# A planner's rule for two engines that share a way into memory, a shorter mask, a scalar add and a split last copy

## The chip, the cores and the metric

The kernel runs on one core of a Trainium2 chip. A core has a matrix engine (TensorE, in the profile PE, with its weight loads as PEld), VectorE (DVE), ScalarE (ACT), GpSimd (POOL) and SyncE (SP), which here issues all the DMAs. Each engine works through its own queue of instructions in order and waits on semaphores for the others. Operands lie in on-chip memory (SBUF), matmul results in PSUM, which is held as eight banks of 128 x 512 words.

The metric is the device time of one execution in microseconds (us), taken over three runs. Their median before the change is 683.23.

## The reference

Attention with a few sink positions and a sliding window, followed by a two-layer network whose activation is the squared positive part. Batch 4, 8 heads, 768 positions, head size 64; 4 sinks and a window of 128; model size 512, inner size 2048.

```python
scores = scale * np.matmul(q, k.transpose(0, 1, 3, 2))
is_sink = pos[None, :] < int(n_sink)
rel = pos[:, None] - pos[None, :]
in_window = (rel >= 0) & (rel < int(window))
scores = np.where(is_sink | in_window, scores, -1000000000.0)
a = np.exp(scores - np.max(scores, axis=-1, keepdims=True))
a = a / (np.sum(a, axis=-1, keepdims=True) + 1e-09)
attn = np.matmul(a, v)
...
x = attn.transpose(0, 2, 1, 3).reshape(B * S, H * D)
h = np.maximum(x @ w_in, 0.0)
return (h * h @ w_out)
```

Queries and keys are float32; the network's weights come as 64-bit floats and are unpacked on the chip.

## The kernel before, in words

**Work.** The 3072 rows of tokens are cut into eight chunks of 384 (two to a batch). For each chunk four pairs of heads go through attention, which leaves x as a high part and a low part; then 16 steps of the network follow, each with 12 first products (L824, x by w_in), the activation (L837, L841, L846, L853) and nine second products (L869) into banks that gather the output. Three products stand for one in both layers: high by high, low by high and high by low.

**Weights.** 32 rows of weights (`row_steps`) are each loaded as 128 x 512 pairs of words, made into 32-bit floats by three DVE passes (L318 with one tensor operand, L325 and L332 with two), copied to a high part by ACT (L338), and a low part is taken by a two-operand subtraction (L342) on DVE or POOL, whichever the planner finds sooner. Most of this falls into the first 125 us.

**Attention.** The first eight pairs (`plain`) take scores straight from q and k (L501). The later 24 first split k and q into high and low parts: a one-operand cast of k on DVE (L459), a two-operand subtraction on POOL (L464), a copy of q on ACT (L470), a two-operand subtraction on DVE (L475), then L507. For each block of 128 queries a DVE instruction adds the mask and takes the row's extreme (L484), ACT exponentiates and sums (L490), DVE adds the small term to the sums and inverts (`recip`, L548 and L549), and each block is scaled by a one-operand pass (L556; ACT's form is L554). The sink columns are copied by POOL (L572), and a low part is subtracted by POOL (L570). Early pairs are then turned by PE (L684, L616), later ones by DVE (L714) and a round trip of DMAs; L772 and L776 multiply by v; L788 and L793 write x.

**Masks.** Three masks exist: `mask0` for the first block of a sequence, `mask1` for the second and `maskA` for the others. They are made once from two index ramps of POOL and the two parameters that a DMA brings, by a run of DVE passes (L221 to L257) and one POOL copy.

**Order.** Every step above is added to a planner with the engines that may do it, a cost in us, a rank, what it reads and writes, and the PSUM bank that it takes. `Plan.order` plays the engines' clocks forward and, each time, emits the step that can start soonest, by rank among those within 0.03 us; among engines for one step it takes the one that would end soonest by its queue and cost. The result is only an order: on the chip each engine goes through its list and waits for semaphores. Steps marked "port" on DVE, and every step of POOL, push each other back in that clock: a step may not start before the last such step of the other engine has had half its cost (`SHARE` is 0.5).

```python
if e == "POOL" or "port" in kind:
    t = max(t, port["DVE" if e == "POOL" else "POOL"])
...
if e == "POOL" or "port" in kind:
    port[e] = t + SHARE * cost
```

**End.** `evacuate` copies the output banks to SBUF (L910) and sends them (L923). The last bank goes in two halves, one copied by DVE and one by ACT, into the same SBUF room, and the second copy is made to wait for the first. After its last DMA issue SP reads a flag, and the engines leave the program.

Of the kernel before, what the change touches and what calls it, by code (L numbers as in the profile page):

```python
# [53 lines left out]
class Plan:  # L54
# [45 lines left out]
    def order(self):  # L100
        free = dict(PE=0.0, DVE=5.5, ACT=1.5, POOL=5.0, SP=0.5)
        port, landed, mode, flow = {"DVE": 0.0, "POOL": 0.0}, [], 0, 0.0
        open_ = [n for n, s in enumerate(self.steps) if s["waits"] == 0]
        while open_:
            best = {}
            for n in open_:
# [8 lines left out]
                if e == "POOL" or "port" in kind:  # L115
                    t = max(t, port["DVE" if e == "POOL" else "POOL"])
                best.setdefault(e, []).append((t, s["rank"], n, cost, kind, picks))
# [44 lines left out]
def sink_window_attention_moe(  # L162
# [25 lines left out]
    with ExitStack() as fast:  # L188
# [23 lines left out]
        mask1 = wp.tile([P, BAND], F32, name="mask1")  # L212
# [6 lines left out]
        )  # L219
        parf = sb("gl1", [P, 2, 2], F32, "parf")  # L220
# [7 lines left out]
        reli = sb("G0", [P, 2 * P], I32, "reli")  # L228
        nc.gpsimd.iota(reli, pattern=[[-1, 2 * P]], base=P, channel_multiplier=1)
        rel = sb("ob0", [P, 2 * P], F32, "rel")  # L230
        nc.vector.tensor_copy(rel, reli)
        coli = sb("gh1", [P, P], I32, "coli")
        nc.gpsimd.iota(coli, pattern=[[1, P]], base=0, channel_multiplier=0)
        col = sb("f0", [P, P], F32, "col")
        nc.vector.tensor_copy(col, coli)

        inw = sb("ob1", [P, 2 * P], F32, "inw")
        nc.vector.tensor_scalar(inw, rel, win, None, op0=ALU.is_lt)
        ge = sb("f1", [P, 2 * P], F32, "ge")
        nc.vector.tensor_scalar(ge, rel, 0.0, None, op0=ALU.is_ge)  # L240
        nc.vector.tensor_tensor(inw, inw, ge, op=ALU.mult)
        snk = sb("f2", [P, P], F32, "snk")
        nc.vector.tensor_scalar(snk, col, ns, None, op0=ALU.is_lt)

        def additive(dst, src):
            nc.vector.tensor_scalar(dst, src, -1.0, BIG, op0=ALU.add, op1=ALU.mult)

        either = sb("G1", [P, P], F32, "either")
# [44 lines left out]
        def bank(key):  # L293
            return banks[plan.got[key]]
# [588 lines left out]
        def evacuate(c, f0, f1, t, okey, n):  # L883
# [9 lines left out]
            if c == NCHUNK - 1 and t == NQ - 1:  # L893
                halves = [slice(0, DM // 2), slice(DM // 2, DM)]
# [311 lines left out]
```

## Time and profile before

| | |
|---|---|
| median of three runs | 683.23 us (682.70 to 684.23) |
| the profiled execution's own time | 682.0 us |
| its span in the profile | 679.8 us |
| PE busy | 659.6 us, 97% |
| DVE busy | 460.5 us, 68% |
| ACT busy | 374.1 us, 55% |
| POOL busy | 211.9 us, 31% |
| first 10 us, PE busy | 4.97 us |

The profile shows one execution. Shares over the whole span mix stages: DVE is nearly full up to 125 us and about 60% busy after 205, so the stretches are read one by one. PE's matmuls are pipelined and their ends are modelled. The trace names an instruction by its line, its engine and the tiles that it writes and reads, then its shape; "x" is a count, and in grouped rows the busy time in us and the mean in ns follow, then the idle time before it and what ended that.

### The profile page before, as it was taken

How to read it: one execution, taken by the hardware profiler on the slowest of the kernel's cores; microseconds unless marked ns; L12 is line 12 of the kernel's file. 1: busy time of each engine (PE TensorE's matmuls, PEld its weight loads, DVE VectorE, ACT ScalarE, POOL GpSimd, SP SyncE). 2: the span in 40 equal slices, each digit the busy share in tenths (PEclk: the TensorE clock that was granted, in tenths of full speed). 3: DMA queues.
4: the chain of work that ended last, by engine and by line, in shares of the span. 5: the costliest groups of instructions: out<-in, count | busy, mean ns of one | idle time of the engine just before them, and what ended most of it. 6: DMA issues, size and time to landing. Idle time of an engine off the chain costs nothing.

```text
span 679.8 us, 11460 instructions
## 1 busy us (share of the span) xinstructions
PE 659.6 (97%) x3662; PEld 573.2 (84%) x3662; DVE 460.5 (68%) x1221; ACT 374.1 (55%) x1070; POOL 211.9 (31%) x383
## 2 busy tenths in 40 slices
PE   5999899999999999999999999999999999999996
PEld 4667788898888888988888898888889888899985
DVE  7999999878888676666667666666767754242221
ACT  5887543356454444556666666666657565542221
POOL 3646443244444333223234422323332331000000
PEclk9999999999999999999999999999999999999999
DMA  7957567016868543466556767546547754310001
GB/s 242 251 168 196 174 206 218 1 37 181 243 179 226 164 133 113 126 206 187 172 153 189 220 181 219 160 144 200 171 159 210 204 164 135 124 62 1 1 0 52
DMA packets 62549, 104.93 MB, mean 154 GB/s; under 512 B 10800, under 2 KB 39216, under 8 KB 62480
## 3 DMA queue, kind: packets, MB, share of 16 engines
q1 hardware_dynamic: 62480, 104.11, 52.0%
q8 instruction: 31, 0.51, 0.3%
q14 instruction: 38, 0.31, 0.1%
HBM read 78.72 MB, written 24.38 MB: 152 GB/s over the span
## 4 chain that ended last, share of the span: by engine, by line
PE 84%; DVE 10%; ACT 2%; DMA 2%; issue 1%; POOL 1%; SPq 0%; DVEq 0%; ACTq 0%
PE bank L869 36%; PE bank L824 35%; PE bank L772 5%; PE bank L507 5%; DVE f L332 2%; DVE f L325 2%; PE bank L776 1%; PE bank L501 1%; DMA PT<-via 1%; DVE P L484 1%; DVE f L318 1%; DVE bank L846 1%; DVE w L342 1%; DVE gl L853 1%; PE bank L684 1%
## 5 line engine op out<-in xcount | busy, mean ns | idle before, releaser
L824 PE MATMUL bank<-x,w 128*128 128x384 f32 x1536 | 301.8, 338 | 0.6 <-DVE gl L853 0.6
L824 PEld LDWEIGHTS bank<-x,w 128*128 128x128 f32 x1536 | 265.9, 188 | 8.9 <-issue 1.0
L869 PE MATMUL bank<-w,gh 128*128 128x512 f32 x768 | 242.5, 397 | 0.5 <-DVE ob L910 0.5
L869 PEld LDWEIGHTS bank<-w,gh 128*128 128x128 f32 x768 | 138.8, 188 | 23.2 <-issue 1.4
L869 PE MATMUL bank<-w,gl 128*128 128x512 f32 x384 | 152.1, 396 | 0.3 <-DVE gl L853 0.3
L464 POOL TENSOR_TENSOR KS<-kn,KS 128x396 fp32r<-128x396 f32 (+1 forms) x48 | 65.0, 1355 | 238.4 <-DVE KS L459 200.8
L837 ACT ACTIVATE r<-bank 128x384 f32<-128x384 f32 x128 | 62.5, 489 | 123.3 <-PE bank L824 122.2
L846 DVE TENSOR_TENSOR bank<-bank,r 128x384 f32<-128x384 f32 x128 | 71.9, 562 | 81.0 <-ACT r L837 80.6
L490 ACT ACTIVATE P<-P,nbs 128x260 f32<-128x260 f32 (+1 forms) x192 | 93.7, 488 | 58.5 <-DVE nbs L484 57.3
L556 POOL TENSOR_SCALAR P<-P,small 128x260 f32<-128x260 f32 (+1 forms) x169 | 84.6, 516 | 63.7 <-DVE small L549 47.4
L869 PEld LDWEIGHTS bank<-w,gl 128*128 128x128 f32 x384 | 72.1, 188 | 18.1 <-DVE gl L853 1.4
L853 DVE TENSOR_TENSOR gl<-bank,gh 128x384 fp32r<-128x384 f32 x128 | 71.2, 556 | 19.8 <-ACT gh L841 10.6
L484 DVE CUSTOM_DVE_ANT_0 P<-bank,maskA 128x260 f32<-128x260 f32 x128 | 52.7, 419 | 46.5 <-PE bank L507 46.1
L841 ACT ACTIVATE gh<-r 128x384 fp32r<-128x384 f32 x128 | 66.8, 522 | 3.5 <-PE bank L869 1.0
L714 DVE STREAM_TRANSPOSE T<-P 128x384 f32<-128x384 f32 x96 | 45.3, 495 | 25.1 <-POOL P L556 23.7
L507 PEld LDWEIGHTS bank<-KS,QS 128*128 128x128 f32 x288 | 52.3, 188 | 5.8
L507 PE MATMUL bank<-KS,QS 128*128 128x260 f32 (+1 forms) x288 | 55.1, 277 | 0.0
L342 POOL TENSOR_TENSOR w<-f,w 128x512 fp32r<-128x512 f32 x20 | 29.6, 1481 | 44.5 <-ACT w L338 38.6
L788 ACT CAST x<-bank 128x384 fp32r<-128x384 f32 x32 | 15.2, 475 | 48.0 <-PE bank L776 47.9
L772 PE MATMUL bank<-PT,vn 128*64 128x256 f32 (+1 forms) x392 | 39.5, 341 | 0.9 <-DMA PT<-via 0.9
L548 DVE TENSOR_TENSOR small<-small,eps 128x3 f32<-128x3 f32 (+1 forms) x56 | 37.1, 662 | 2.9 <-ACT P L490 2.1
L772 PEld LDWEIGHTS bank<-PT,vn 128*64 128x64 f32 x392 | 25.2, 136 | 16.2 <-issue 5.7
(100 smaller groups left out, 551.5 us busy)
## 6 DMA issues: line engine op xcount, KB each, us to landing
raw<-in_moe_w_dram SPq DMA_DIRECT2D x32, 512.0 KB, 4.2
half<-in_moe_w_dram SPq DMA_DIRECT2D x64, 256.0 KB, 3.7
via<-T SPq DMA_DIRECT2D x48, 192.0 KB, 3.1
PT<-via SPq DMA_DIRECT2D x12, 768.0 KB, 4.5
via<-T SPq DMA_DIRECT2D x48, 160.0 KB, 2.8
PT<-via SPq DMA_DIRECT2D x12, 640.0 KB, 4.9
kn<-in_k_dram SPq DMA_DIRECT2D x24, 264.0 KB, 4.2
qn<-in_q_dram SPq DMA_DIRECT2D x32, 192.0 KB, 3.0
```

The costliest lines, as they stand in the source:

```text
L464: lambda h=h: nc.gpsimd.tensor_tensor(KS(h)[:, 1, 0:nk], kn()[:, h, 0:nk], f32(KS(h)[:, 0, 0:nk]), op=ALU.subtract),
L484: nc.vector.tensor_tensor_reduce(Pt(h)[:, i, o : o + n], ps_[:, 0:n], mask[:, 0:n], -SCALE, BIG, ALU.add, ALU.min, nb)
L490: nc.scalar.activation(Pt(h)[:, i, o : o + n], Pt(h)[:, i, o : o + n], AF.Exp, bias=nb, scale=-1.0, accum_out=sm[:, h, i : i + 1],)
L507: nc.tensor.matmul(bank(key)[:, 0:n], QS(h)[:, cols], flat[:, a, c0 : c0 + n], start=(a == 0), stop=(a == 1),)
L556: {"POOL": nc.gpsimd, "DVE": nc.vector}[engine].tensor_scalar(a, a, rs[:, h, i : i + 1], 1.0, op0=ALU.mult, op1=ALU.mult)
L772: nc.tensor.matmul(xo[h * D : h * D + D, qs[0] * P : qs[0] * P + len(qs) * P], vn[:, kk, h, :], rhs(), start=(n == 0), stop=False, skip_gr ...
L824: nc.tensor.matmul(bank(key)[:, 0:TOK], wi[fc][:, i, cc * P : (cc + 1) * P], xt[:, cc, :], start=(cc == 0 and j == 0), stop=(cc == NCC - 1 ...
L837: lambda key=key, r=r: nc.scalar.activation(r(), bank(key)[:, 0:TOK], AF.Relu),
L841: ("ACT", 0.41), n - 9, lambda gh=gh, r=r: nc.scalar.activation(gh(), r(), AF.Square),
L846: lambda key=key, r=r: nc.vector.tensor_tensor(bank(key)[:, 0:TOK], bank(key)[:, 0:TOK], r(), op=ALU.mult),
L853: lambda key=key, gh=gh, gl=gl: nc.vector.tensor_tensor(gl(), bank(key)[:, 0:TOK], f32(gh()), op=ALU.subtract),
L869: nc.tensor.matmul(bank(okey), gt()[:, ts_], wo[f][:, i, :], start=(f == f0 and j == 0), stop=(f == f1 - 1 and j == 2),)
```

## The change

Five things are changed.

- In the planner, "port" now marks two-operand passes alone, of DVE and of POOL. These exclude each other for their whole cost. A POOL step without the mark waits until half of the last marked DVE step has gone; it holds nobody. The one-operand steps of DVE (L318, L390, L459, L556, L610) lose the mark, POOL's subtractions (L342, L464, L570) get it, and some costs are changed.
- The small term is added as a constant by a one-operand pass, and the tile that held it and its memset go.
- The index ramps and what needs no parameter are computed ahead of the parameters' first use. The window's two comparisons become one two-operand instruction, the sink test and the union another; `mask1` is written first, its two big parts by one instruction, and POOL copies it to `maskA`, whose four sink columns are then written over.
- The two halves of the last output go to two different rooms of SBUF, so the second copy no longer waits for the first.
- A marked DVE step now keeps two times, one for POOL's marked steps and one (`half`) for the others.

```diff
-                if e == "POOL" or "port" in kind:
+                if "port" in kind:
                     t = max(t, port["DVE" if e == "POOL" else "POOL"])
+                elif e == "POOL":
+                    t = max(t, half)
...
-                if e == "POOL" or "port" in kind:
-                    port[e] = t + SHARE * cost
+                if "port" in kind:
+                    port[e] = t + cost
+                    if e == "DVE":
+                        half = t + SHARE * cost
...
-        eps = wp.tile([P, 2 * NQ], F32, name="eps")
-        nc.gpsimd.memset(eps, EPS)
...
+        reli = sb("G0", [P, 2 * P], I32, "reli")
+        nc.gpsimd.iota(reli, pattern=[[-1, 2 * P]], base=P, channel_multiplier=1)
+        coli = sb("gh1", [P, P], I32, "coli")
+        nc.gpsimd.iota(coli, pattern=[[1, P]], base=0, channel_multiplier=0)
+        rel = sb("ob0", [P, 2 * P], F32, "rel")
+        nc.vector.tensor_copy(rel, reli)
+        ge = sb("f1", [P, 2 * P], F32, "ge")
+        nc.vector.tensor_scalar(ge, rel, 0.0, None, op0=ALU.is_ge)
+        col = sb("f0", [P, P], F32, "col")
+        nc.vector.tensor_copy(col, coli)
...
-        nc.vector.tensor_scalar(inw, rel, win, None, op0=ALU.is_lt)
...
-        nc.vector.tensor_tensor(inw, inw, ge, op=ALU.mult)
-        snk = sb("f2", [P, P], F32, "snk")
-        nc.vector.tensor_scalar(snk, col, ns, None, op0=ALU.is_lt)
...
+        nc.vector.scalar_tensor_tensor(inw_, rel, win, ge, op0=ALU.is_lt, op1=ALU.mult)
         either = sb("G1", [P, P], F32, "either")
-        nc.vector.tensor_tensor(either, inw[:, P : 2 * P], snk, op=ALU.max)
+        nc.vector.scalar_tensor_tensor(either, col, ns, inw[:, 1], op0=ALU.is_lt, op1=ALU.max)
         additive(mask0, either)
-        additive(maskA[:, 0:P], inw[:, 0:P])
-        additive(maskA[:, P:BS], snk[:, 0:NS])
-        additive(maskA[:, BS:BAND], inw[:, P : 2 * P])
-        nc.gpsimd.tensor_copy(mask1, maskA)
+        snk = sb("f2", [P, NS], F32, "snk")
+        nc.vector.tensor_scalar(snk, col[:, 0:NS], ns, None, op0=ALU.is_lt)
         only = sb("gh0", [P, NS], F32, "only")
-        nc.vector.tensor_tensor(only, snk[:, 0:NS], inw[:, 0:NS], op=ALU.is_gt)
+        nc.vector.tensor_tensor(only, snk, inw[:, 0, 0:NS], op=ALU.is_gt)
+        additive(mask1_[:, :, 0:P], inw)
         additive(mask1[:, P:BS], only)
+        nc.gpsimd.tensor_copy(maskA, mask1)
+        additive(maskA[:, P:BS], snk)
...
-                ("DVE", 0.345, "port"), rank,
+                ("DVE", 0.345), rank,
...
-                [("DVE", 0.62, "port", LOW_DVE), ("POOL", 1.3)], rank, low, reads=[f_cell, ("w", n)], writes=[("wl", n)]
+                [("DVE", 0.62, "port", LOW_DVE), ("POOL", 1.28, "port")], rank, low, reads=[f_cell, ("w", n)], writes=[("wl", n)]
...
-                        ("DVE", 0.35, "port"), r,
+                        ("DVE", 0.35), r,
...
-                        ("POOL", 1.35 if nk == 4 else 1.25), r,
+                        ("POOL", 1.33 if nk == 4 else 1.06, "port"), r,
...
-                        ("DVE", 0.6, "port"), r,
+                        ("DVE", 0.55, "port"), r,
...
-                nc.vector.tensor_tensor(rs[:, hs], sm[:, hs], eps.rearrange("p (h i) -> p h i", h=2)[:, hs], op=ALU.add)
+                nc.vector.tensor_scalar(rs[:, hs], sm[:, hs], EPS, None, op0=ALU.add)
...
-                    ("DVE", 0.22), r - URGE, lambda hs=hs: recip(hs),
+                    ("DVE", 0.27), r - URGE, lambda hs=hs: recip(hs),
...
-                        pool = ("POOL", 0.46 if n > P else 0.33)
+                        pool = ("POOL", 0.47 if n > P else 0.37)
...
-                                ("DVE", 0.25 if n > P else 0.18, "port", SC_DVE),
+                                ("DVE", 0.25 if n > P else 0.18, "", SC_DVE),
...
-                        ("POOL", 0.29), r - URGE + 0.01, lambda h=h: part_sinks(h, False),
+                        ("POOL", 0.2), r - URGE + 0.01, lambda h=h: part_sinks(h, False),
...
-                        ("POOL", 0.32), r - URGE + 0.01, lambda h=h: part_sinks(h, True),
+                        ("POOL", 0.2, "port"), r - URGE + 0.01, lambda h=h: part_sinks(h, True),
...
-                    [("ACT", 0.4), ("DVE", 0.35, "port", CP_DVE)], rank(0.8) - URGE,
+                    [("ACT", 0.4), ("DVE", 0.35, "", CP_DVE)], rank(0.8) - URGE,
...
+            rest = lambda: sb("T", [P, DM], F32, "ob_rest")
...
-                        )(ob()[:, cols], bank(okey)[:, cols]),
-                        reads=[okey] + [cell] * (x > 0),
-                        writes=[cell] if len(halves) == 1 else [(cell, x)] + [cell] * (x == 0),
+                        )((rest() if x else ob())[:, cols], bank(okey)[:, cols]),
+                        reads=[okey], writes=["T" if x else cell],
...
-                        nc.sync.dma_start(out=out[r0 : r0 + P, cols], in_=ob()[:, cols])
+                        nc.sync.dma_start(out=out[r0 : r0 + P, cols], in_=(rest() if x else ob())[:, cols])
...
-                    reads=[cell] if len(halves) == 1 else [(cell, x)],
+                    reads=["T" if x else cell],
```

More of the change, by code (lines that the diff above doesn't have):

```diff
@@ L101, in order @@
         free = dict(PE=0.0, DVE=5.5, ACT=1.5, POOL=5.0, SP=0.5)
-        port, landed, mode, flow = {"DVE": 0.0, "POOL": 0.0}, [], 0, 0.0
+        port, landed, mode, flow, half = {"DVE": 0.0, "POOL": 0.0}, [], 0, 0.0, 0.0
         open_ = [n for n, s in enumerate(self.steps) if s["waits"] == 0]
@@ L211, in sink_window_attention_moe @@
         maskA = wp.tile([P, BAND], F32, name="maskA")
-        mask1 = wp.tile([P, BAND], F32, name="mask1")
+        mask1_ = wp.tile([P, 2, BS], F32, name="mask1")
+        mask1 = mask1_.rearrange("p a c -> p (a c)")[:, 0:BAND]
         mask0 = wp.tile([P, P], F32, name="mask0")
-        eps = wp.tile([P, 2 * NQ], F32, name="eps")
-        nc.gpsimd.memset(eps, EPS)
         pari = sb("gl0", [P, 2, 2], I32, "pari")
@@ L226, in sink_window_attention_moe @@
         ns, win = par[:, 0:1], par[:, 1:2]
[L228 to L241, printed above, removed]
-        snk = sb("f2", [P, P], F32, "snk")
-        nc.vector.tensor_scalar(snk, col, ns, None, op0=ALU.is_lt)
         def additive(dst, src):
             nc.vector.tensor_scalar(dst, src, -1.0, BIG, op0=ALU.add, op1=ALU.mult)
+        inw = sb("ob1", [P, 2, P], F32, "inw")
+        inw_ = inw.rearrange("p a c -> p (a c)")
+        nc.vector.scalar_tensor_tensor(inw_, rel, win, ge, op0=ALU.is_lt, op1=ALU.mult)
         either = sb("G1", [P, P], F32, "either")
-        nc.vector.tensor_tensor(either, inw[:, P : 2 * P], snk, op=ALU.max)
+        nc.vector.scalar_tensor_tensor(either, col, ns, inw[:, 1], op0=ALU.is_lt, op1=ALU.max)
         additive(mask0, either)
-        additive(maskA[:, 0:P], inw[:, 0:P])
-        additive(maskA[:, P:BS], snk[:, 0:NS])
-        additive(maskA[:, BS:BAND], inw[:, P : 2 * P])
-        nc.gpsimd.tensor_copy(mask1, maskA)
+        snk = sb("f2", [P, NS], F32, "snk")
+        nc.vector.tensor_scalar(snk, col[:, 0:NS], ns, None, op0=ALU.is_lt)
         only = sb("gh0", [P, NS], F32, "only")
-        nc.vector.tensor_tensor(only, snk[:, 0:NS], inw[:, 0:NS], op=ALU.is_gt)
+        nc.vector.tensor_tensor(only, snk, inw[:, 0, 0:NS], op=ALU.is_gt)
+        additive(mask1_[:, :, 0:P], inw)
         additive(mask1[:, P:BS], only)
+        nc.gpsimd.tensor_copy(maskA, mask1)
+        additive(maskA[:, P:BS], snk)
         wchk = wp.tile([P, 2, 2 * NROW], F32, name="wchk")
@@ L389, in sinks @@
             add(
-                ("DVE", 0.35, "port"), rank, lambda: nc.vector.tensor_copy(VS[0:rows], raw()),
+                ("DVE", 0.35), rank, lambda: nc.vector.tensor_copy(VS[0:rows], raw()),
                 reads=VR, writes=["VS"],
@@ L909, in evacuate, with send @@
                         on if len(halves) == 1 else (on[0], 0.35), n - 0.5,
-                        lambda on=on, cols=cols: (
+                        lambda on=on, cols=cols, x=x: (
                             nc.scalar.copy if on[0] == "ACT" else nc.vector.tensor_copy
-                        )(ob()[:, cols], bank(okey)[:, cols]),
-                        reads=[okey] + [cell] * (x > 0),
-                        writes=[cell] if len(halves) == 1 else [(cell, x)] + [cell] * (x == 0),
+                        )((rest() if x else ob())[:, cols], bank(okey)[:, cols]),
+                        reads=[okey], writes=["T" if x else cell],
                         drop=[okey],
                     )
-                def send(cols=cols):
+                def send(cols=cols, x=x):
                     if f1 < NFC:
```

## The prediction

> **What bounds the kernel now.** I read the span and the busy shares first, then busy times by stretch, then the chain of waits in order of time, and last the groups of the stretch in which TensorE (PE) still idles.
>
> ```profile
> span 679.8 us, 11460 instructions
> 10.00:20.00 10.00, 6.71 (x45) 4.55 (x41) 9.84 (x38) 8.56 (x32) 5.00 (x11) 1.00 1.01 311
> 20.00:60.00 40.00, 38.82 (x256) 27.84 (x255) 39.41 (x116) 33.95 (x96) 23.32 (x45) 1.00 0.72 208
> 60.00:80.00 20.00, 17.68 (x108) 14.33 (x107) 19.13 (x37) 14.02 (x32) 11.05 (x13) 1.00 0.56 182
> 80.00:125.00 45.00, 44.18 (x228) 38.73 (x227) 43.29 (x75) 18.79 (x36) 16.36 (x11) 1.00 0.58 176
> 125.00:190.00 65.00, 65.00 (x360) 57.95 (x360) 50.29 (x143) 33.53 (x92) 24.82 (x49) 1.00 0.47 130
> 190.00:205.00 15.00, 14.13 (x90) 11.96 (x89) 12.99 (x40) 8.69 (x27) 8.42 (x16) 1.00 0.65 176
> 205.00:668.00 463.00, 463.00 (x2546) 409.62 (x2545) 276.82 (x736) 250.28 (x739) 119.01 (x223) 1.00 0.50 147
> ```
>
> After the stretch and its length the columns are PE, PE's weight loads, VectorE (DVE), ACT and POOL, then the granted clock, which is 1.00 throughout. PE's idle time is length less busy: 3.29 us in 10 to 20, 1.18 in 20 to 60, 2.32 in 60 to 80, 0.82 in 80 to 125, none in 125 to 190, 0.87 in 190 to 205, none for the 463 us after. That is 8.48 us between 10 and 668. PE's work isn't touched by the change, so whatever a new order does from 10 us on, it can give back 8.48 us at most, 1.2% of the span. DVE is full (39.41 of 40) just where PE is nearly full too: it is not DVE alone that bounds 20 to 125, and a microsecond off DVE isn't a microsecond off the end.
>
> ```profile
> 2.29 3.46 DMA kn<-in_k_dram
> 5.79 4.74 PE bank L501 x20
> 10.53 0.41 DVE P L484
> ...
> 4.39 0.16 DVE L225 SCALAR_TENSOR_TENSOR par<-parf,neg 128x2 f32<-128x2 f32 x1
> 4.80 0.35 DVE L238 TENSOR_SCALAR inw<-rel,par 128x256 f32<-128x256 f32 x1
> 5.46 0.42 DVE L241 TENSOR_TENSOR inw<-inw,ge 128x256 f32<-128x256 f32 x1
> 6.64 0.29 DVE L484 CUSTOM_DVE_ANT_0 P<-bank,mask 128x128 f32<-128x128 f32 x1
> 7.44 0.43 DVE L484 CUSTOM_DVE_ANT_0 P<-bank,mask 128x260 f32<-128x260 f32 x1
> ```
>
> The chain (its first three rows here) begins with the load of keys, runs over 20 score matmuls of PE without a break, and enters DVE only at 10.53. The five rows below are DVE's own timeline over the mask steps: they lie beside the load and those matmuls.
>
> **Masks in fewer steps: 0.0 us (bounds -1.1 and 0).** Three casts and comparisons move ahead of the parameters' arrival, two two-step masks become one instruction each, two mask slices become one. From `par` (4.39) to the first 260-wide reduction (7.44) there are 3.05 us now. Of what follows `par` after the change, a 256-wide two-operand pass, three of 128 to 256 elements and four tiny ones stay, some 1.4 us going by the rows' starts, and two 128-wide reductions of some 0.25 each: about 1.9, so 1.1 less. But DVE is again waiting for PE at 10.53, so what it gains early it would spend waiting; I take 0. The new wait is in front of the last small mask op: POOL's copy must precede it, and behind it in DVE's queue stand the reductions, which ACT's exponentials await. Today the same wait, for a copy in the other direction, lies between the two reductions after 6.64 and the one at 7.44; now that copy starts earlier, so I add nothing.
>
> **The small term as a scalar: 0.0 us (bounds -0.9 and 0).**
>
> ```profile
> L548 DVE TENSOR_TENSOR small<-small,eps 128x3 f32<-128x3 f32 x48 | 35.8, 746 | 2.9 <-ACT P L490 2.1
> L548 DVE TENSOR_TENSOR small<-small,eps 128x6 f32<-128x6 f32 x8 | 1.2, 155 | 0.0
> L464 POOL TENSOR_TENSOR KS<-kn,KS 128x528 fp32r<-128x528 f32 x24 | 35.2, 1469 | 116.5 <-DVE KS L459 99.1 <-DMA out_dram<-ob 8.6 <-DMA via<-T 7.4
> ```
>
> This add takes 155 ns on six columns but 746 on three: in the later stage it is held up behind POOL's long key pass. Freed, 48 x (746 - 155) = 28 us of DVE time go. If the one-operand form is held just the same, nothing goes; no row shows a three-column one-operand pass under a POOL pass. Either way its cover is PE, which has no idle in 125 to 190 nor after 205; the only place without cover is 190 to 205, 0.87 us. POOL's memset of the term at the start is off every path.
>
> **Last halves in two rooms: 0.0 us (bounds -0.1 and 0).**
>
> ```profile
> 673.56 0.37 ACT L910 COPY ob<-bank 128x256 f32<-128x256 f32 x1 [0.56 <-DVE ob L910]
> 673.02 1.55 SPq L923 DMA_DIRECT2D out_dram<-ob  x3
> ```
>
> ACT's copy of the second half waits for DVE's copy of the first and would now start some 0.5 us earlier. But the three last output DMAs are issued back to back from 673.02 to 674.57, 0.52 each: SP's queue, not ACT, holds the last one, and the program's end comes after that queue. ACT's wait is covered by two issues of 0.52; were SP free it would be worth 0.5.
>
> **The planner's new rules: -1.0 us.** The planner only fixes each engine's order. What it believed was that every POOL pass and every marked DVE pass keep the other away for half their cost. Now the two-operand ones exclude each other for the whole cost, POOL's one-operand passes wait for half a DVE two-operand pass but hold nobody, and DVE's one-operand passes (L318, L390, L459, the scalings L556, sink copies L610) are free. What the trace says of it:
>
> ```profile
> L332 DVE SCALAR_TENSOR_TENSOR f<-raw,f x32: 653/684/1731, 17.6 to 127.6; 128x512 int32<-128x512 int32 x32
> L332 DVE SCALAR_TENSOR_TENSOR f<-raw,f 128x512 int32<-128x512 int32 x32 | 29.4, 926 | 0.2
> L325 DVE SCALAR_TENSOR_TENSOR f<-raw,f x32: 651/681/1792, 16.1 to 125.3; 128x512 int32<-128x512 int32 x32
> L325 DVE SCALAR_TENSOR_TENSOR f<-raw,f 128x512 int32<-128x512 int32 x32 | 23.4, 742 | 0.0
> L318 DVE TENSOR_SCALAR f<-raw x32: 410/418/1224, 15.4 to 124.3; 128x512 int32<-128x512 int32 x32
> L318 DVE TENSOR_SCALAR f<-raw 128x512 int32<-128x512 int32 x32 | 14.9, 484 | 0.0
> L342 POOL TENSOR_TENSOR w<-f,w 128x512 fp32r<-128x512 f32 x20 | 29.6, 1481 | 44.5 <-ACT w L338 38.6 <-DMA qn<-in_q_dram 5.9
> 122.83 1.29 POOL L342 TENSOR_TENSOR w<-f,w 128x512 fp32r<-128x512 f32 x1 [1.28 <-ACT w L338]
> 123.19 1.22 DVE L318 TENSOR_SCALAR f<-raw 128x512 int32<-128x512 int32 x1
> ```
>
> Sum less 32 medians is the time these passes were held: L332 29.4 - 21.9 = 7.5 us, L325 23.4 - 21.8 = 1.6, L318 14.9 - 13.4 = 1.5, together 10.6. PE's idle in 20 to 60 and 80 to 125, where the rows are unpacked and DVE sets the pace, is 1.18 + 0.82 = 2.0, so a microsecond of such holding has cost PE about 0.19 (estimate from these rows). If the full exclusion takes away half of the 9.1 us of two-operand holding, that is -0.9. Half, because the hold is only as good as the planner's clock (it costs L342 at 1.28, the row has 1.48), and because DVE must have other work ready. Bounds: 0 and -2.0.
>
> L318 is the other side. In the last two rows it starts 0.36 after a POOL two-operand pass and takes 1.22 for 0.42: it is held to that pass's end like a two-operand one. The new rules call it free, so it will be put there more often. If its 1.5 us doubles, the same 0.19 gives +0.3; bounds 0 and the +2.3 of the second rival.
>
> [...]
>
> Next, POOL's small subtractions of the sink columns (L570), which now exclude DVE's two-operand passes:
>
> ```profile
> 14.70 1.15 POOL L570 TENSOR_TENSOR PSK_wide<-P,PSK_wide 128x8 fp32r<-128x8 f32 x2
> 14.70 0.74 DVE L395 SCALAR_TENSOR_TENSOR VS<-VS,third,vs 24x512 fp32r<-24x512 f32 x1
> 15.90 0.44 PE L616 MATMUL bank<-ident,PSK_wide 128*128 128x128 f32 x2 [0.74 <-POOL PSK_wide L570]
> ```
>
> Here the second of two is held behind L395 and PE idles 0.74 for it. I take half, -0.4 (0 to -0.74), since L318 comes next in DVE's queue and may take L395's place as the holder.
>
> Then the query's low pass (L475) must now wait for the whole of L464 (1469 ns) instead of half. It belongs to the later pairs, almost wholly under PE's full stretches: 0.0; without cover +0.7 (the third rival). New costs of a few hundredths (a scaling 0.33 to 0.37) may move a scaling between POOL, ACT and DVE: no sign, 0.
>
> Sum: 0 + 0 + 0 - 0.9 + 0.3 - 0.4 = -1.0 us. The profiled execution took 682.0 (span 679.8 and 2.2 around it); the median of the runs is 683.23, 1.2 above it. I put the sum on the median: **682.2**.
>
> **Rivals.** First, *the order gets much cleaner* (faster). All of the 2.0 us goes, all 0.74 of L570, and half of the 2.32 in 60 to 80:
>
> ```profile
> 70.57 2.84 POOL L556 TENSOR_SCALAR P<-P,small 128x260 f32<-128x260 f32 x3
> 71.58 0.96 DVE L318 TENSOR_SCALAR f<-raw 128x512 int32<-128x512 int32 x2
> 72.46 1.48 DVE L325 SCALAR_TENSOR_TENSOR f<-raw,f 128x512 int32<-128x512 int32 x2
> 73.36 1.26 POOL L572 CAST PSK_wide<-P 128x24 fp32r<-128x24 f32 x2
> 75.02 0.33 PE L616 MATMUL bank<-ident,PSK_wide 128*128 128x128 f32 x1 [2.32 <-POOL PSK_wide L570]
> ```
>
> That is -3.9: **679.3**. For it: the largest idle of PE is one accident of order, POOL's scalings starved by DVE passes in a row, and any new order redraws it. Against: the rule for POOL's one-operand passes, which are what starves here, stays half a pass.
>
> Second, *one-operand passes stacked on POOL's* (slower). The same picture a second time: with L318 and the scalings free and DVE's two-operand passes no longer held by POOL's scalings, a pair's POOL chain (three scalings, two casts, two subtractions) meets holding DVE passes again. It decides from the point where PE has no products ready: then it costs what 75.02 shows, +2.3: **685.5**. For it: L318 at 123.19, and the stack of two L318 and two L325 above. Against: from 80 on, PE has products to run and the eight early pairs are nearly over.
>
> Third, *key passes hold the query's low pass* in the one later stretch where PE idles (190 to 205, 0.87): half of 1469 more, +0.7 on no gain: **683.9**.
>
> **How the numbers follow.** Chances: forecast 0.40, first rival 0.34, second 0.20, third 0.06. What this kernel's runs can tell from no change is 0.2%, 1.37 us: below 681.86 is faster, above 684.60 slower. The forecast's own range is 681.0 to 683.8, and I count 0.08 of its 0.40 below 681.86. Faster: 0.34 + 0.08 = 0.42; same: 0.32 + 0.06 = 0.38; slower 0.20. The range reaches past the first rival by half a microsecond and just to the second: 678.8 to 685.6.
>
> **What would show it.** Right: PE's idle in 10 to 205 falls from 8.48 to some 7.5; L332's mean falls from 926 towards 800, L318's rises above 484; DVE reaches the 260-wide reduction before 7.44 but the chain still enters DVE near 10.5; the last three output DMAs still issue back to back. L548's mean near 155 or still near 746 shows whether the add was freed, with PE full either way. Wrong: an idle of PE over 2 us anywhere before 125, or any in 205 to 668, or an end that follows ACT's last copy.

## The result: slower by 5 us

The changed kernel takes 687.82 us (median of five executions, 686.14 to 689.49) against 682.85 for the kernel before (682.31 to 684.23): a ratio of 1.0071, 95% interval 1.0048 to 1.0095. The forecast was 682.2, the range 678.8 to 685.6.

The profiled execution took 689.09 us. In the changed kernel's file most lines lie two further down (L318 is L320, L332 is L334, L548 is L550, L744 is L746); the last copies and sends, L910 and L923, are L913 and L925. First the busy time by stretch, the view that the prediction began with; after the stretch and its length the columns are PE, PEld, DVE, ACT and POOL, the granted clock, the DMA share and GB/s.

```profile
span 687.3 us, 11468 instructions
10.00:20.00 10.00, 8.57 (x45) 5.44 (x41) 9.87 (x39) 8.42 (x32) 4.98 (x12) 0.83 0.96 301
20.00:60.00 40.00, 37.34 (x235) 26.55 (x235) 37.16 (x108) 29.07 (x82) 18.25 (x36) 0.96 0.60 183
60.00:80.00 20.00, 19.15 (x117) 14.55 (x114) 19.93 (x48) 14.70 (x39) 10.19 (x16) 1.00 0.57 170
...
205.00:240.00 35.00, 31.36 (x174) 25.78 (x173) 22.71 (x62) 14.33 (x40) 13.16 (x24) 0.95 0.66 179
```

and of the kernel before the same stretch from 205:

```profile
205.00:240.00 35.00, 35.00 (x202) 30.74 (x201) 26.79 (x72) 16.76 (x44) 12.01 (x22) 1.00 0.68 199
```

Two things differ. PE idles 35.00 - 31.36 = 3.64 us in 205 to 240, where it had no idle before. And the granted clock, 1.00 in every stretch of the execution profiled before, is 0.83, 0.96 and 0.95 in three stretches: (1 - 0.83) x 10, (1 - 0.96) x 40 and (1 - 0.95) x 35 are 1.7, 1.6 and 1.75 us of PE's time, so "busy" no longer means the same work. All of PE's idle from 10 to 668 is 8.85 us (1.43, 2.66, 0.85 and 3.64 in these rows, 0.27 in those left out, none after 240), against 8.48 before: the sum hardly moved, and yet the span grew by 7.5.

It did not grow before 205. There the idle fell from 8.48 to 5.21 us while 3.3 us of clock are missing, which cancel, and by 205 PE has issued 384 products of the network's first layer and 272 of its second, against 381 and 270 before, and 15 fewer of attention's shorter ones: it is about level. By 240 it has issued 444 and 321, against 463 and 333: 31 fewer, some 6 us of PE's work (twelve of the first took 2.12 us, nine of the second 2.11). So the loss lies in 205 to 240, whose idle and missing clock make 3.64 + 1.75 = 5.4; 0.6 more lie behind PE's last product, from whose end to the end of the span it is 7.4 us, before 6.7.

A clock short of 1.00 is not new with the change, though. The profiled execution before had a mean clock of 0.998; 25 other executions of that kernel had 0.991 to 0.998, on average 0.9946, and the five of the changed kernel 0.986 to 0.994, on average 0.9908. The profiled pair therefore shows more of the clock than the medians hold: the missing clock differs by some 2.6 us on average (estimate from these means), not by 5.

**The clock.** The same view in stretches of 2 us:

```profile
12.00:14.00 2.00, 1.18 (x8) 0.54 (x5) 1.97 (x10) 1.75 (x8) 1.16 (x3) 1.00 0.91 307
14.00:16.00 2.00, 1.62 (x11) 0.87 (x11) 2.00 (x8) 1.17 (x2) 1.28 (x5) 0.86 0.99 395
16.00:18.00 2.00, 2.00 (x12) 1.33 (x12) 1.97 (x7) 1.93 (x8) 0.54 (x1) 0.50 1.07 312
18.00:20.00 2.00, 1.76 (x9) 0.89 (x6) 1.97 (x7) 1.57 (x5) 2.00 (x5) 0.79 0.98 229
...
220.00:222.00 2.00, 1.77 (x9) 1.17 (x11) 1.12 (x4) 0.31 (x2) 1.11 (x3) 0.56 0.57 191
222.00:224.00 2.00, 2.00 (x14) 1.67 (x11) 0.12 (x1) 0.28 (x1) 1.92 (x4) 0.59 0.99 194
```

From 14 to 20 the missing clock is 2 x (0.14 + 0.50 + 0.21) = 1.7 us, from 220 to 224 it is 2 x (0.44 + 0.41) = 1.7: each time half of a stretch of 3.4 us. The first runs from 15.44 to 18.85, at 0.50 throughout. Each follows a time with idle of PE in it, but with work as well: PE was busy for 2.80 of the 4 us from 12 to 16 (2.21 of the 3.41 up to 15.44, where the halving begins), for 2.54 of the 3.4 us from 39.2 to 42.6, ahead of the halved stretch that ends at 46, and for 1.01 of the 3.41 up to 220.19, ahead of the last one. How little work brings a halving on, these rows don't show.

**The wait at 217.5.** Rows of SP, PE and DVE in the timeline:

```profile
210.93 0.78 SPq L430 DMA_DIRECT2D qn<-in_q_dram  x1
212.82 0.33 SPq L746 DMA_DIRECT2D PT<-via  x1
213.24 1.36 SPq L425 DMA_DIRECT2D kn<-in_k_dram  x2
...
219.59 0.08 DVE L486 DVE_READ_ACCUMULATOR2_ANT nbs<- 128x1 f32 x1
220.23 2.83 PE L774 MATMUL bank<-PT,vn 128*64 128x256 f32 x16 [2.44 <-DVE nbs L486]
```

The gather's row in the list of transfers; its last number is us from issue to landing:

```profile
PT<-via SPq DMA_DIRECT2D x1, 768.0 KB, 7.3
```

The releaser named is DVE's L486, but that had ended at 219.67. The gather of turned probabilities (L746), which these products multiply, was issued at 212.82 and took 7.3 us: it landed at 220.1, and PE starts 0.1 later. In the same list of the kernel before it took 4.2:

```profile
PT<-via SPq DMA_DIRECT2D x1, 768.0 KB, 4.2
```

In the kernel before, SP's rows have a query load and two key loads behind the gather and none of them just ahead of it:

```profile
208.69 0.34 SPq L744 DMA_DIRECT2D PT<-via  x1
209.12 0.67 SPq L423 DMA_DIRECT2D kn<-in_k_dram  x1
209.91 0.52 SPq L428 DMA_DIRECT2D qn<-in_q_dram  x1
210.48 0.65 SPq L423 DMA_DIRECT2D kn<-in_k_dram  x1
```

**The holding.** DVE's groups after the change (busy us, mean ns | idle before):

```profile
L550 DVE TENSOR_SCALAR small<-small 128x3 f32<-128x3 f32 x48 | 30.7, 639 | 4.3 <-ACT P L492 3.3
L327 DVE SCALAR_TENSOR_TENSOR f<-raw,f 128x512 int32<-128x512 int32 x32 | 23.5, 744 | 0.0
L334 DVE SCALAR_TENSOR_TENSOR f<-raw,f 128x512 int32<-128x512 int32 x32 | 23.1, 726 | 0.1
L320 DVE TENSOR_SCALAR f<-raw 128x512 int32<-128x512 int32 x32 | 19.9, 635 | 0.0
L461 DVE CAST KS<-kn 128x528 fp32r<-128x528 f32 x24 | 12.2, 507 | 0.8 <-DMA kn<-in_k_dram 0.8
```

Two events of DVE under POOL passes, from the timeline:

```profile
38.27 1.31 POOL L344 TENSOR_TENSOR w<-f,w 128x512 fp32r<-128x512 f32 x1 [4.51 <-ACT w L340]
38.50 1.11 DVE L550 TENSOR_SCALAR small<-small 128x6 f32<-128x6 f32 x1
...
208.66 1.34 POOL L466 TENSOR_TENSOR KS<-kn,KS 128x528 fp32r<-128x528 f32 x1 [0.53 <-DVE small L550]
208.73 1.56 DVE L461 CAST KS<-kn 128x528 fp32r<-128x528 f32 x1
```

L334's mean fell from 926 to 726 ns, so its held time (sum less 32 medians of 0.684) went from 7.5 to 1.2 us. L320's rose from 484 to 635: 19.9 - 32 x 0.418 = 6.5 us held, where it was 1.5. For the three unpacking passes together it is 9.4 after 10.6: the holding moved from the two-operand passes to the one-operand pass. The pairs of rows show it elsewhere: an add of six columns, 155 ns on average before, takes 1.11 us under L344, and the cast of keys, 428 before, takes 1.56 under L466.

**Start and end.** The last copies and sends, from the timeline:

```profile
679.29 2.12 SPq L925 DMA_DIRECT2D out_dram<-ob  x3
...
680.40 0.37 ACT L913 COPY ob_rest<-bank 128x256 f32<-128x256 f32 x1 [0.56 <-DVE ob L913]
681.50 0.40 SPq L925 DMA_DIRECT2D out_dram<-ob_rest  x1
```

ACT's copy still begins when DVE's has ended, with 0.56 us of idle as before, though it writes to another room; SP issues without a break. At the start the 260-wide reduction comes at 7.16 instead of 7.44, and the chain of waits still enters DVE behind PE's 20 matmuls, at 10.62 (5.88 + 4.74).

### The profile page after: what moved, and what is told of

It is laid out like the page before. It is cut to its first block, busy times and chain, and to the rows that moved or that the text cites. A ratio compares the mean times of both kernels' runs of the same rounds, so it can differ in the third digit from the quotient of the medians.

```text
span 687.3 us, 11468 instructions
## 1 busy us (share of the span) xinstructions
PE 665.9 (97%) x3662; PEld 576.1 (84%) x3662; DVE 458.5 (67%) x1225; ACT 372.1 (54%) x1066; POOL 209.5 (30%) x380
## 4 chain that ended last, share of the span: by engine, by line
PE 88%; DVE 6%; issue 2%; POOL 1%; DMA 1%; ACT 1%; SPq 0%; DVEq 0%; ACTq 0%
PE bank L826 37%; PE bank L871 37%; PE bank L774 5%; PE bank L509 4%; PE bank L503 1%; PE bank L778 1%; DVE P L486 1%; POOL P L558 1%; PE bank L686 1%; DVE P L558 1%; DVE f L320 1%; DMA kn<-in_k_dram 1%; ACT P L492 0%; DVE f L327 0%; DVE bank L848 0%
## 5 line engine op out<-in xcount | busy, mean ns | idle before, releaser
L466 POOL TENSOR_TENSOR KS<-kn,KS 128x396 fp32r<-128x396 f32 (+1 forms) x48 | 63.2, 1317 | 224.8 <-DVE KS L461 216.4
L558 POOL TENSOR_SCALAR P<-P,small 128x260 f32<-128x260 f32 (+1 forms) x164 | 85.3, 534 | 68.4 <-DVE small L551 55.5
L486 DVE CUSTOM_DVE_ANT_0 P<-bank,maskA 128x260 f32<-128x260 f32 x128 | 52.5, 418 | 49.2 <-PE bank L509 47.8
L344 POOL TENSOR_TENSOR w<-f,w 128x512 fp32r<-128x512 f32 x23 | 31.5, 1371 | 61.6 <-ACT w L340 56.4
L774 PE MATMUL bank<-PT,vn 128*64 128x256 f32 (+1 forms) x392 | 41.9, 356 | 2.4 <-DVE nbs L486 2.4
L550 DVE TENSOR_SCALAR small<-small 128x3 f32<-128x3 f32 (+1 forms) x56 | 33.3, 595 | 4.5 <-ACT P L492 3.6
```

Source lines behind the costliest of these rows:

```text
L466: lambda h=h: nc.gpsimd.tensor_tensor(KS(h)[:, 1, 0:nk], kn()[:, h, 0:nk], f32(KS(h)[:, 0, 0:nk]), op=ALU.subtract),
L486: nc.vector.tensor_tensor_reduce(Pt(h)[:, i, o : o + n], ps_[:, 0:n], mask[:, 0:n], -SCALE, BIG, ALU.add, ALU.min, nb)
L558: {"POOL": nc.gpsimd, "DVE": nc.vector}[engine].tensor_scalar(a, a, rs[:, h, i : i + 1], 1.0, op0=ALU.mult, op1=ALU.mult)
L774: nc.tensor.matmul(xo[h * D : h * D + D, qs[0] * P : qs[0] * P + len(qs) * P], vn[:, kk, h, :], rhs(), start=(n == 0), stop=False, skip_gr ...
```

## The experiments

Theory A: the planner's new rules take DVE's one-operand passes for free and set them under POOL's, where they are held; the orders that come of it lose time. Rivals: any of the other edits, any redrawn order, or the clock by itself. Each ratio is to the kernel before, measured on the same chip, with its 95% interval.

**The planner alone, and the rest alone.** The first kernel is the one before with the diff's lines in `Plan.order`, the marks and the costs; the second is the changed kernel without them.

> The kernel before with the planner's edits alone (rules, marks and costs); masks, small term and last halves as before. Theory A (the new rules treat VectorE's one-operand passes as free, set them under GpSimd's passes, and PE's stalls and half-clock stretches follow from that order): 687.8 +- 1.5 us, that is slower by 3 to 6 us; L318's mean (484 ns before) 600 ns or more; at least two stretches of 3.41 us at a granted clock of 0.5. Theory B (the other edits matter): 684.5 us or less, no such stretch.

> The changed kernel with the planner's edits undone: masks in fewer steps, small term as a scalar and last halves in two rooms alone. Theory A (the loss is the planner's): 682.9 +- 0.8 us, the same as before, no half-clock stretch after 12 us, and the mean of the scalar add on three columns is still 600 to 750 ns, since the one-operand form is held too. Theory B (one of these edits redraws the start or the sums for the worse): 685 us or more.

The planner's edits alone: 685.87 us, ratio 1.0041 (1.0024 to 1.0058), between the two times expected; L318's group is at 634 ns, PE idle 35.00 - 32.62 = 2.38 us in 205 to 240, one halved stretch (a clock of 0.98 and 0.96 in 10 to 20 and 20 to 60) where two were expected. The rest alone: 684.38 us, 1.0011 (1.0001 to 1.0020), so 0.8 us and not nothing, and again between the two times expected. The planner carries most of the loss, 0.0041 of 0.0071; the two parts do not add up to the whole.

In the second kernel the order is nearly that of before, and the scalar add (its line there is 546) can be compared with the 746 ns of the two-operand add. Its group, and one row of the busy times by stretch:

```profile
L546 DVE TENSOR_SCALAR small<-small 128x3 f32<-128x3 f32 x48 | 35.8, 747 | 3.1 <-ACT P L488 2.4
```

```profile
60.00:80.00 20.00, 17.67 (x100) 14.57 (x99) 18.91 (x37) 13.71 (x32) 10.95 (x13) 0.91 0.58 181
```

747 against 746: the form makes no difference, the pass is held as long as the two-operand form. The stretch row may hold the 0.8, which one execution can't show: PE's idle of 2.33 is that of before, but here the clock is halved behind it (0.91).

**The marks back on DVE's one-operand passes**, under the new exclusion for the whole cost.

```diff
-                ("DVE", 0.345), rank,
+                ("DVE", 0.345, "port"), rank,
...
-                    ("DVE", 0.27), r - URGE, lambda hs=hs: recip(hs),
+                    ("DVE", 0.27, "port"), r - URGE, lambda hs=hs: recip(hs),
```

and so for the casts (L392, L461), the scalings (L558) and the sink copies (L612). `recip` (L550, L551) had no mark in the kernel before either, so that one is new and not put back.

> The changed kernel with VectorE's one-operand passes (L320, the cast of vs, the cast of keys, the scalings, the sink copies, the sum's add) marked again as ones that exclude GpSimd's, now for the whole of their cost. Theory A (it is these unmarked passes that are held): L320's mean falls from about 620 ns to 500 or less, no more than one half-clock stretch, 681.5 to 684.5 us. Theory B (the full exclusion of the two-operand passes, or any redrawn order, is what hurts): 686 to 689 us.

682.76 us, 0.9984 (0.9976 to 0.9993): the whole loss is gone, 0.0087 of ratio from the changed kernel. Its groups and its stretch from 205:

```profile
L550 DVE TENSOR_SCALAR small<-small 128x3 f32<-128x3 f32 x48 | 21.8, 453 | 1.8 <-ACT P L492 1.6
L320 DVE TENSOR_SCALAR f<-raw 128x512 int32<-128x512 int32 x32 | 15.9, 511 | 0.0
```

```profile
205.00:240.00 35.00, 34.60 (x198) 30.12 (x197) 25.52 (x67) 15.78 (x41) 12.25 (x22) 1.00 0.72 193
```

L320 is at 511 (500 was expected) and PE idles 0.40. Its clock is 0.92 in 10 to 20 and 0.94 in 20 to 60, so 3.2 us are missing, two stretches and not one at most, and yet it is the faster kernel: a count of halved stretches by itself says little. Theory A's time came true and Theory B's, 686 to 689, did not.

**Only the late marks, only the early ones.** The late: L461, and `recip` (L550, L551). The early: L320, L392, L558, L612.

> The changed kernel with only the later stage's one-operand passes marked again as excluding GpSimd's: the cast of keys (L461) and the sum's add and reciprocal (L550, L551). Theory L (the loss comes from the later stage's passes, placed under GpSimd's key passes): L550's mean falls from 639 towards 450 ns, PE has under 1 us of idle in 205 to 240 (4.8 in the changed kernel), 684.5 us or less. Theory U (it comes from the unpacking passes, L320, and is carried on as lateness): L320's mean stays at 600 ns or more and the time at 686 to 689 us.

> The changed kernel with only the early stage's one-operand passes marked again: L320, the cast of vs, the scalings on VectorE and the sink copies. Theory U (the unpacking passes): L320's mean falls from 635 to 520 ns or less, and the time to 684.5 us or less. Theory L (the later stage's passes): 686 to 689 us with L550's mean still near 640 ns.

Late marks: 685.91 us, 1.0029 (1.0015 to 1.0042). Early marks: 688.20, 1.0064 (1.0042 to 1.0086). The rows of 205 to 240, late marks and then early marks:

```profile
205.00:240.00 35.00, 34.60 (x203) 29.69 (x202) 24.50 (x67) 15.49 (x42) 13.55 (x24) 1.00 0.72 189
```

```profile
205.00:240.00 35.00, 31.67 (x175) 26.07 (x174) 22.71 (x63) 14.61 (x41) 13.17 (x24) 0.95 0.67 182
```

The late marks take the loss after 205 away (0.40 of idle against 3.33 with the early marks), and they alone bring the time down. Theory L's numbers came true (L550 at 443 ns with late marks, and with early ones at 651 and 688.20 us) but for the time of the late marks, 685.91 instead of 684.5 or less: there L320 stays at 672 ns, as Theory U had it, and PE idles 45.00 - 42.11 = 2.89 in 80 to 125, where the changed kernel has 0.05, so a loss before 205 takes the place of half the gain. Neither set is enough by itself. Whether the mark on L461 or the new one on `recip` clears the late loss was not tried.

**The clock by filling.** Matmuls of the identity, overwritten later, are put on PE where it idles; trace rows count each twice (x44 for 22 of them in the last kernel below).

```diff
+                        for _ in range(fill):
+                            nc.tensor.matmul(bank(key_t)[:, 0:P], ident, ident, start=True, stop=True)
                         for h, kk, qs, off in blocks:
```

> The changed kernel with a few idle-time matmuls of a 128x128 identity added on PE (6 ahead of the first turn of pair s=0, 3 ahead of that of s=4, 2 ahead of each head's sink transposes of both; their products are overwritten), in the stretches where PE streams little at 12 to 15 and at 39 to 43 us. Theory A2 (the clock is halved for 3.41 us after a stretch in which PE did little): the half-clock stretches at 15.4 and at 42.8 vanish, the one at 220.2 stays, about 3.4 us less than the changed kernel, 684.4 +- 1.2 us. Theory C (the halving is not a matter of PE's work): stretches stay, 687.8 us or a little more.

687.44 us, 1.0050 (1.0037 to 1.0063), against the changed kernel's 1.0071: the expected 3.4 us less would be 1.0021, which this interval leaves out (the changed kernel's own, 1.0048 to 1.0095, aside). In the profiled execution both early stretches are gone, as A2 said, and the late one stays:

```profile
14.00:16.00 2.00, 2.00 (x19) 1.63 (x19) 2.00 (x7) 1.37 (x3) 1.19 (x5) 1.00 0.96 383
...
220.00:222.00 2.00, 2.00 (x13) 1.47 (x10) 0.44 (x1) 0.00 (x0) 2.00 (x4) 0.50 0.66 146
```

That fits a halving that follows PE's own work, but one execution shows little: the kernel with the key loads moved (below) has a clock of 1.00 in both early stretches without any filler. Nor does the run settle what a stretch is worth. Over five executions each the mean clock rose from 0.9908 to 0.9942 only, some 2.3 us, not 3.4, and the ratios differ by 0.0021, some 1.4 us. The next kernel added score matmuls ahead of the wait at 217.5.

> The run with added identity matmuls at 12 and at 39 us (687.44 us), and besides, six extra pairs of score matmuls on PE just ahead of its wait at 217.5 us (the same scores again, overwritten), so that the stretch from 216.5 to 220 holds some 1.4 us more of streaming. If a half-clock stretch costs half its length where PE is what sets the pace: the stretch at 220 goes, about 1.7 us less than that run, 685.8 +- 0.8 us. If it costs nothing there either: 687.4 +- 0.8 us. PE's wait for the gather stays.

687.33 us, 1.0037 (1.0023 to 1.0050): against 1.0050 this fits a gain of 1.7 us (0.0025) and one of nothing alike, so it settles nothing by its time. In its profiled execution the clock is 1.00 in 205 to 240, so the late stretch is gone, but 3.6 us of clock are missing in 20 to 60, in spite of the early fillers:

```profile
20.00:60.00 40.00, 38.47 (x236) 27.08 (x236) 36.73 (x104) 28.38 (x80) 17.28 (x33) 0.91 0.58 176
```

The halved stretches lie elsewhere from one profiled execution to the next (20 to 60 at 1.00 with the early fillers alone, at 0.91 here), and the fillers at these fixed places of the program clear them in some of them only.

**The gather's neighbours.** Everything in the order of the changed kernel, but two key loads on SP, which follow the gather by 0.4 us, go behind the two output transfers (steps 1326 and 1327 are these loads, 1134 is the second transfer).

```diff
+                n = plan.log[-1][4]
+                if n in (1326, 1327):
+                    held.append(emit)
+                    continue
                 emit()
+                if n == 1134:
+                    for late in held:
+                        late()
```

> The changed kernel in its own order, but for two transfers on SP: the two key loads that follow the gather of turned probabilities at 212.8 us (L425 behind L746) go behind the two output transfers that came after them. Theory D (the gather took 7.3 us from issue to landing, not 4.2, since the key loads ran beside it, and PE waited 2.6 us for it): it lands in 4.2 to 5.0, PE's wait at 217.5 falls below 0.8, the half-clock stretch at 220 goes, 683.5 to 685 us. Theory O (the pair is late as a whole: bank releases and the sums hold PE there just the same): PE's wait stays over 1.5 us, 686.5 to 688.5 us.

> The run with added identity matmuls at 12 and at 39 us together with the key loads moved behind the two output transfers. If the two causes add (the key loads beside the gather; the half-clock stretches, which in the run with the key loads moved alone set its slow executions apart): 684 +- 0.8 us with all executions within 2 us of each other. If the spread of 6 us of that run has another cause: median 685 or more, spread over 4 us.

Key loads moved: 685.21 us, 1.0024 (1.0008 to 1.0040), just above the 683.5 to 685 expected; twelve executions from 683.1 to 689.1. These go with the clock: 683.81 and 684.17 us where the execution's mean clock is 0.998, 686.83, 687.02 and 689.10 where it is 0.991 or less. PE's wait for the gather fell from 2.4 to 0.7 us, but the gather took 6.5 us there, not 4.2 to 5.0. With the fillers as well: 686.22, 1.0036 (1.0022 to 1.0050): the two do not add, and the expected 684 was missed. There the gather was issued at 212.65, as in the changed kernel, and took 5.9; the key loads therefore account for 7.3 - 5.9 = 1.4 us of it (0.8 by the 6.5). The rest pointed at the query load, 1.9 us ahead of the gather, so it was moved as well (step 1325).

> The changed kernel in its own order, but the query load that SP issues 1.9 us ahead of the gather of turned probabilities (L430 at 210.9) and the two key loads behind that gather all go behind the two output transfers. If the gather's 7.3 us came from these two neighbours: it lands in 4.2 to 4.8 us (5.9 to 6.5 with the key loads moved alone), PE's wait before the gather's products is below 0.4 us, 683 to 685 us in executions without an early half-clock stretch. If the transfer of turned probabilities ahead of it, or something else, slows it: 5.5 us or more.

The list of transfers and PE's waits from 205 to 240:

```profile
PT<-via SPq DMA_DIRECT2D x1, 768.0 KB, 4.2
```

```profile
PE bank L871 <- DVE ob L906: 1.2, 1, 1.2
PE bank L826 <- DVE gl L855: 0.4, 1, 0.4
```

4.2 us, as before the change, and PE no longer waits for it: the neighbours were the cause. The other kernels fit: where the query load goes out 1.9 us ahead of this gather and both key loads behind it, it took 6.8 us or more (6.8 with the planner's edits alone, 6.9 with the early marks); where the query load comes behind it, 4.2 before the change, 4.8 with all marks and 5.7 with the late ones. Key loads behind the gather are thus not enough by themselves to make it take 7.3. A new wait takes part of the gain, 1.2 us for a copy of an output bank. The time is 685.78 us, 1.0033 (1.0018 to 1.0047): about half of the changed kernel's 1.0071 goes. The three executions with the highest clock, 0.996, took 683.63, 684.10 and 684.53 us, within the 683 to 685 expected of executions without an early halved stretch, and the four with the lowest, 0.990 and 0.991, 685.77 to 687.74. By its median it is no better than with the key loads moved alone, whose interval overlaps.

**All passes exclude each other for the whole cost.** To the kernel with all marks back:

```diff
                 elif e == "POOL":
-                    t = max(t, half)
+                    t = max(t, port["DVE"])
...
-                if "port" in kind:
+                if e == "POOL" or "port" in kind:
                     port[e] = t + cost
```

and, as a separate kernel, the one before with one constant changed:

```diff
-SHARE = 0.5
+SHARE = 1.0
```

> The kernel of the run with all VectorE one-operand passes marked again (682.76 us), in which GpSimd's one-operand passes (scalings, casts of sink columns) and VectorE's marked passes now exclude each other for the whole cost too. Theory A (a plan that is nearer to the chip gives a better order): L327's and L334's means fall from 821 and 762 to 740 ns or less, 681.5 to 682.7 us. Rival (so much exclusion leaves VectorE idle where it sets the pace): 683.2 us or more.

> The kernel before with one constant changed: the share of a pass's cost for which the planner keeps the other engine's passes away is 1 and not a half, for all of GpSimd's passes and all marked VectorE passes; no other part of the change. If the gain of the run in which all exclude each other (680.92 us) comes from that rule: 680.5 to 682.3 us. If the change's other edits (costs, masks, last halves) are needed for it: 683 us or more.

680.92 us, 0.9955 (0.9940 to 0.9969), and 679.44, 0.9936 (0.9923 to 0.9950): both faster than either kernel, the second by one constant, and both below even the faster times expected. Of the two means named for the first only L327's fell, to 741 ns; L334's rose to 805, and L320's fell to 420. A stretch of the second:

```profile
20.00:60.00 40.00, 40.00 (x268) 29.46 (x268) 36.38 (x109) 33.06 (x98) 20.22 (x37) 0.94 0.64 187
```

PE has no idle in 20 to 60, where before it had 1.18; its clock lacks 0.06 x 40 = 2.4 us there. Less holding is not what this kernel gains by: its three unpacking passes take 26.0, 25.7 and 14.5 us, 66.2 together against 67.7 before. Nor does PE's idle account for the gain: from 10 us on it is 6.58 us (5.55 of it in 10 to 20) against 8.48, 3.5 us of clock are missing, and yet the span is 2.5 shorter. So part of what counts as PE's busy time before was not full work, and how the new order saves it is open.

**The clock where PE sets the pace.** Both of these have a halved stretch in which PE is busy, and a last pair of kernels fills PE's idle ahead of it.

> The run in which all passes exclude each other for the whole cost (680.92 us) with 25 added identity matmuls on PE in its idle between 11.5 and 20.5 us, where that run has PE at half clock from 15.7 to 25.9. If PE sets the pace in 20.5 to 26: full clock there, 1 to 2.7 us less, 678.2 to 679.9 us. If DVE sets it, as in the changed kernel at 12 and 39 us: 680.9 +- 0.5 us.

> The kernel before with the planner's share at 1 (679.44 us), with 27 identity matmuls added on PE in its idle at 15 and from 16.2 to 19.5 us (overwritten later). That run has PE at half clock from 17.9 to 24.7 and busy throughout 20 to 60. If a half-clock stretch costs half its length where PE is what sets the pace: full clock from 19.6 on, 2.0 to 2.6 us less, 676.8 to 677.8 us. If it costs little there either: 679.4 +- 0.7 us.

The first: 679.36 us, 0.9932 (0.9918 to 0.9945), from 0.9955: within what was expected. The second: 678.55, 0.9933 (0.9920 to 0.9947) from 0.9936, less than expected, and by the ratios no gain that the noise lets one see. The fillers did act on the clock: with them its mean is 0.996 or more in all ten executions of the two kernels, without them 0.993 or less in all eleven. So in these two kernels the clock follows PE's own work. PE's timeline shows why the second gains so little. Without the fillers (SHARE at 1):

```profile
19.56 1.16 PE L684 MATMUL bank<-ident,P 128*128 128x128 f32 x4 [3.35 <-DVE P L556]
...
21.39 2.40 PE L772 MATMUL bank<-PT,vn 128*64 128x128 f32 x12
...
28.77 0.39 PE L776 MATMUL bank<-SK,VS 128*128 128x256 f32 x1
```

With them:

```profile
16.12 5.08 PE L683 MATMUL bank<-ident 128*128 128x128 f32 x44
21.03 0.60 PE L688 MATMUL bank<-ident,P 128*128 128x128 f32 x4
...
21.99 1.30 PE L776 MATMUL bank<-PT,vn 128*64 128x128 f32 x12
...
27.81 0.39 PE L780 MATMUL bank<-SK,VS 128*128 128x256 f32 x1
```

The same twelve products take 1.30 instead of 2.40, and the work from the first row to the last is done in 27.81 - 21.03 = 6.78 instead of 9.21 us: 2.43 us, against (24.7 - 19.56) x 0.5 = 2.6 of missing clock, since PE is at half clock until 24.7 there. Here, where PE sets the pace, a halved stretch costs nearly half its length, as forecast. But the fillers themselves ran past PE's idle, and the work began 1.47 later. The net is the 0.9 us by which the profiled spans differ (677.3 and 676.4).

## Why the prediction was wrong, point by point

- **The step that failed** is the first one, which bounded everything else: "PE's work isn't touched by the change, so whatever a new order does from 10 us on, it can give back 8.48 us at most". It was meant for the gain and was used as if it bounded the loss. Two things passed it by. The 463 us after 205 without idle were taken as cover for everything in them, and what the change does to the later pairs was priced at 0.0 for it; but they were the result of one order. The new one has 3.64 us of idle and 1.75 of missing clock in 205 to 240, for a late gather, and is 31 products of the network behind at 240 where it was about level at 205. And PE's speed is not fixed: its clock is halved for 3.4 us at a time, and its mean is lower after the change than before (0.9908 against 0.9946).
- **Two-operand passes, -0.9.** The holding did go, more of it than the half that was taken (L332's group from 7.5 to 1.2 us). No such gain was seen in the time: PE's idle in 20 to 60 and 80 to 125, from which the term was worked out, went from 2.00 to 2.71 us.
- **L318 unmarked, +0.3.** The mechanism was right, its size was not: the holding was to double from 1.5 us and went to 6.5. The same happened to the cast of keys (428 to 507 ns on average) and the add of six columns (155 to 329), which the sum priced at nothing. Marking all of them again took 0.0087 of ratio away, some 6 us.
- **POOL's small subtractions, -0.4.** The wait that was priced, 0.74 us at 15.90, is 0.21 after (PE's L618 at 15.34), so it went by a little more than the half taken. The first rival's large idle, 2.32 us in 60 to 80, is 0.85 after. Both gains are seen in the idle and neither in the time.
- **Small term as a scalar, 0.0.** Right, by the bound "if the one-operand form is held just the same, nothing goes"; it is held, 747 against 746 ns in the old order (639 in the new one).
- **Masks, 0.0, and last halves, 0.0.** The signs named for both came: the 260-wide reduction earlier, the chain unmoved, SP back to back. That ACT's copy would start 0.5 sooner was wrong; it still waits for DVE's, though the room is another, and what makes it wait is open. The three small edits together measured 1.0011, not 1.0000.
- **The rivals.** The second had the mechanism, one-operand passes stacked on POOL's passes, but looked for it in POOL's chain of the early pairs, at +2.3 us. It came in the later pairs, by way of SP's order and a DMA, beyond the range. The third named the late stage and priced it by the 0.87 us idle of 190 to 205. That the rules for POOL's one-operand passes were too weak, said against the first rival, was right: with these also exclusive the time is 680.92.
- **Open.** Before 205 a smaller idle and more missing clock cancel in the profiled execution; how much of the median's 5 us is the clock's was not told apart from the order's, since the fillers' times moved by less than the intervals. How the unmarked late passes lead the planner to that order around the gather is open too; that the loss after 205 comes with them is shown by the kernels with late and with early marks. No kernel redraws the order by something that has nothing to do with the marks, so how far orders differ by accident isn't known; the small edits alone moved the time by 0.8 us.

## What to carry to other kernels

A planner that fixes an order can pay for a wait that it doesn't know, and not only where that wait is: here the whole cost of exclusion for all passes of POOL and all marked ones of DVE is worth 0.64% (0.9936), and leaving it out for the short, one-operand ones costs more (0.0087) than the rule for the others brings. PE's idle before says nothing of what an order can lose, and it is no strict measure of what one can gain, since a busy PE need not be at full work (with the share at 1 the idle fell by 1.9 us and the span by 2.5, under a worse clock); a stretch without idle is the work of the present order, so look for which transfers keep it fed and what the new order sets beside them. When a stall names a releaser that had long ended, look up the landing of the transfers that the waiting instruction reads.

## What the runs showed of the hardware that was not expected

- The PE clock was halved for 3.4 us (0.50 from 15.44 to 18.85 in the changed kernel) behind 3.4 us in which PE was busy for 2.2. Where a halving lands differs from one profiled execution to the next (20 to 60 at a granted 0.96 in the changed kernel, at 1.00 with the early fillers and at 0.91 with all of them). Its price was nearly half its length where PE sets the pace (2.43 us of work for 2.6 of missing clock). In the kernel with the key loads moved the executions at a mean clock of 0.998 took 683.8 and 684.2 us, those at 0.991 or less 686.8 to 689.1.
- One gather of 768 KB took 4.2 us or 7.3, by what SP issued 1.9 us ahead of it (a query load of 192 KB) and 0.4 us behind it (two key loads of 264 KB each): 5.9 to 6.5 without the latter, 4.2 without either, and 4.2 in the kernel before, with one key load 0.4 us behind it and the other two loads 1.2 and 1.8 us behind.
- An add over three columns is held behind a POOL pass like any large one (747 ns on average, where six columns took 155 before the change), and in its one-operand form as long as in its two-operand form.
